# Where the inverse roots of a normalisation are worked out: on 112 x 4 numbers and spread by products, or on all 128 x 448 at once

## The chip, the cores and the metric

The kernel runs on one core of one Trainium2 chip. The metric is the device time of one execution in microseconds (us), median over several runs. TensorE multiplies matrices and writes its sums to PSUM; VectorE, ScalarE and GpSimd work element by element (GpSimd not in PSUM); SyncE issues the transfers. Every engine takes its instructions strictly in the order in which the program lists them, and waits at an instruction whose input or output buffer is not ready.

## The reference, cut to what matters

Three stages follow one another: a sigmoid attention with 4 batches of 448 tokens and 12 heads, a gated feed-forward block with a root-mean-square normalisation in front (768 to 1536 to 768), and a routed block with 8 experts. The change lies in the normalisation.

```python
def _moe_ref(x, w_gate, w_val, w_out, rms_g):            # x: 1792 tokens x 768
    rms = np.sqrt(np.mean(x * x, axis=-1, keepdims=True) + 1e-06)
    xn = x / rms * rms_g
    g = xn @ w_gate
    silu = g * (1.0 / (1.0 + np.exp(-g)))
    val = xn @ w_val
    return (silu * val @ w_out)
```

## The kernel before, in words

One batch of 448 tokens is one step of the whole. Activations stand with their features on the partitions and the tokens along a row: `xt` is six tiles of 128 x 448. Each token therefore needs one factor, 1 / root of its mean square, and that factor has to stand on all 128 partitions before a tile can be multiplied by it.

The feed-forward block of batch b (`moe1(b)`) is written as 72 pieces of nine products each: 48 pieces for gate and value, then 24 pieces for the six output chunks, four pieces to a chunk. One chunk is 36 products into one PSUM bank (lines 297, 298, 299: each value and each weight is split into a high and a low part, and three of the four partial products are taken). After every piece one step of the attention of batch b + 1 is put into the program (`attention_due`), and `later(n, ...)` puts work n pieces further on. The order on every engine is thus fixed by the code, and nothing is reordered at run time.

In the output chunks these instructions belong together. Each chunk leaves PSUM through line 338 (ScalarE, high part `x2s`), line 341 (VectorE, low part) and line 344 (VectorE, a transposed copy, the last reader of the bank). The logits (line 383, two short products) read both parts one chunk later. The next weights are split by line 250 (ScalarE, `wh`) and line 253 (VectorE, `wl`), two pairs per chunk, and line 299 reads `wl`. While batch 0 is in `moe1`, VectorE also turns 64-bit weight words into 32-bit ones (lines 219, 223, 227).

The attention of a batch ends with the normalisation, which for batches 1 to 3 lies beside the output chunks of the batch before it: about 200 to 230 us (first place), 378 to 405 us (second place) and 552 to 579 us (third place). Batch 0 has its own, at 50 us. The sums of squares per partition are in `ss` (128 x 448). Four products with `ss` as the stationary operand and a column of ones add over the partitions and leave 112 x 4 sums (`pm`, line 773). VectorE makes a first guess of 1 / root from the bits (lines 778 to 786); three Newton steps follow, by GpSimd for batches 1 to 3 (lines 793 to 796). VectorE copies the 112 x 4 factors 128 times side by side (`yb`, line 801), and four products with an identity matrix bring them to all partitions in PSUM (`prs`, line 805). Line 814 multiplies the six tiles, line 817 (ScalarE) takes the high part and line 808 (VectorE) the low part.

Of the kernel before, what the change touches and what calls it, by code (L numbers as in the profile page):

```python
# [9 lines left out]
F32 = mybir.dt.float32  # L10
F32R = mybir.dt.float32r
F16 = mybir.dt.float16
I32 = mybir.dt.int32
AF = mybir.ActivationFunctionType
ALU = mybir.AluOpType
# [4 lines left out]
B, H, S, D = 4, 12, 448, 64  # L20
NT = B * S
DM = H * D
# [6 lines left out]
CT = 112  # L29
NC = S // CT  # L30
# [66 lines left out]
def f32(ap):  # L97
    return ap.bitcast(F32)
# [3 lines left out]
def block_kernel(ctx, tc, qkp, qk, v, wg, wv, wo, g, gate, w1, w2, consts, out):  # L102
    nc = tc.nc
    ctx.enter_context(tc.manual_schedule())

    def opened(name, side="left", **kw):
        s = ExitStack()
        return s, s.enter_context(tc.tile_pool(name=name, bufs=1, side=side, **kw))
# [8 lines left out]
    s_a, aq = opened("aq", side="right", reuse_waits="tile")  # L117
# [6 lines left out]
    def const(name, parts=128):  # L124
        a, n = CONST[name]
        return cst[:parts, a : a + n]

    ident = const("ident")
    ones = cpool.tile([128, 128], F32, name="ones")
# [3 lines left out]
    start = cpool.tile([128, 1], F32, name="start")  # L133
# [15 lines left out]
    def bank(tag, bufs, shape, name):  # L149

        if tag not in fixed:
            return ps.tile(shape, F32, tag=tag, name=name, bufs=bufs)
        t = fixed[tag].pop(0)
        fixed[tag].append(t)
        n = math.prod(shape[1:])
        t = t[: shape[0], :n]
        return t if len(shape) == 2 else t.rearrange("p (a b) -> p a b", b=shape[2])
# [30 lines left out]
    sc_bank = lambda shape, name: bank("sc", 2, shape, name)  # L188
# [351 lines left out]
    def attention(b):  # L540
# [25 lines left out]
        def low(t):  # L566
            h, c = divmod(t, NC)
            a, ah = a_t[t]
            if c == 3:
                nc.vector.tensor_tensor(out=ah[64:128], in0=a[64:128], in1=f32(ah[64:128]), op=ALU.subtract)  # L570
                al = None
            else:
                al = aq.tile([128, S], F32R, tag="al", name="al", bufs=3)
                nc.vector.tensor_tensor(out=al, in0=a, in1=f32(ah), op=ALU.subtract)
            a_t[t] = ah, al
# [162 lines left out]
        for t in range(n_steps + 4 if b > 1 else 0):  # L738
            if t < n_steps:
                h, c = divmod(t, NC)  # L740
# [27 lines left out]
            step()  # L768
            yield

        pm = sc_bank([CT, NC], "pm")
        for c in range(NC):
            nc.tensor.matmul(pm[:, c : c + 1], ss[:, c * CT : (c + 1) * CT], ones[:, 0:1], start=True, stop=True)
        yield
        va = aq.tile([CT, NC], F32, tag="va", name="va")
        ya = aq.tile([CT, NC], F32, tag="ya", name="ya")
        ta = aq.tile([CT, NC], F32, tag="ta", name="ta")
        nc.vector.tensor_scalar(out=va, in0=pm, scalar1=1.0 / DM, scalar2=1e-6, op0=ALU.mult, op1=ALU.add)

        nc.vector.tensor_scalar(  # L780
            out=ta.bitcast(I32), in0=va.bitcast(I32), scalar1=1, scalar2=None, op0=ALU.logical_shift_right
        )
        nc.vector.tensor_scalar(
            out=ya.bitcast(I32), in0=ta.bitcast(I32), scalar1=-1.0, scalar2=float(0x5F3759DF), op0=ALU.mult, op1=ALU.add
        )
        nc.vector.tensor_scalar(out=va, in0=va, scalar1=-0.5, scalar2=None, op0=ALU.mult)
        for _ in range(3):
            if b == 0:
                nc.vector.tensor_tensor(out=ta, in0=ya, in1=ya, op=ALU.mult)
                nc.vector.tensor_tensor(out=ta, in0=ta, in1=va, op=ALU.mult)  # L790
                nc.vector.scalar_tensor_tensor(out=ya, in0=ta, scalar=1.5, in1=ya, op0=ALU.add, op1=ALU.mult)
            else:
                nc.gpsimd.tensor_tensor(out=ta, in0=ya, in1=ya, op=ALU.mult)
                nc.gpsimd.tensor_tensor(out=ta, in0=ta, in1=va, op=ALU.mult)
                nc.gpsimd.tensor_scalar(out=ta, in0=ta, scalar1=1.5, scalar2=None, op0=ALU.add)
                nc.gpsimd.tensor_tensor(out=ya, in0=ya, in1=ta, op=ALU.mult)
        if b > 0:
            yield
            yield
        yb = aq.tile([CT, NC, 128], F32, tag="yb", name="yb")  # L800
        nc.vector.tensor_copy(out=yb, in_=ya.unsqueeze(2).to_broadcast([CT, NC, 128]))
        yield
        pr = sc_bank([128, S], "prs")
        for c in range(NC):
            nc.tensor.matmul(pr[:, c * CT : (c + 1) * CT], yb[:, c, :], ident[:CT, :CT], start=True, stop=True)
        yield
        def low(c, xh, xl):
            nc.vector.tensor_tensor(out=xl, in0=xt[c], in1=f32(xh), op=ALU.subtract)  # L808

# [1 line left out]
        for c in range(KD):  # L811
# [3 lines left out]
                out=xt[c], in0=xt[c], scalar=g_sb[:, c : c + 1], in1=pr, op0=ALU.mult, op1=ALU.mult  # L815
# [366 lines left out]


    att = {b: attention(b) for b in range(B)}
    for n in range(H // 2 * NC + 2):
        next(att[0])
# [6 lines left out]
        if n == 15:  # L1193
            nc.scalar.copy(out=gate_2[:, :, :E], in_=gate_sb)
            nc.vector.tensor_tensor(
                out=gate_2[:, :, E:], in0=gate_sb, in1=f32(gate_2[:, :, :E]), op=ALU.subtract
# [12 lines left out]
    for b in range(B):  # L1209
# [3 lines left out]
        for n, _ in enumerate(moe1(b)):  # L1213
# [5 lines left out]
            if b == 0:  # L1219
                if to_store:  # L1220
                    c, w = to_store.pop(0)
# [186 lines left out]
```

## Time and profile before

| | |
|---|---|
| median of 3 runs | 988.81 us (988.07 to 988.83) |
| the profiled execution | 988.29 us, of it 986.2 us from the first to the last instruction |
| TensorE busy | 963.8 us, 98% |
| VectorE busy | 637.2 us, 65% |
| ScalarE busy | 463.6 us, 47% |
| GpSimd busy | 14.9 us, 2% |
| mean granted TensorE clock | 0.998 of full speed |

Busy shares are averages over stages that are bound in different ways; what a change in one stage does has to be read in that stage. A row of the timeline gives start, duration, engine, line, operation, output and inputs, and in brackets the idle time of the engine ahead of it with what ended it. A product's duration is longer than its distance to the next one, because products overlap.

### The profile page before, as it was taken

How to read it: one execution, taken by the hardware profiler on the slowest of the kernel's cores; microseconds unless marked ns; L12 is line 12 of the kernel's file. 1: busy time of each engine (PE TensorE's matmuls, PEld its weight loads, DVE VectorE, ACT ScalarE, POOL GpSimd, SP SyncE). 2: the span in 40 equal slices, each digit the busy share in tenths (PEclk: the TensorE clock that was granted, in tenths of full speed). 3: DMA queues.
4: the chain of work that ended last, by engine and by line, in shares of the span. 5: the costliest groups of instructions: out<-in, count | busy, mean ns of one | idle time of the engine just before them, and what ended most of it. 6: DMA issues, size and time to landing. Idle time of an engine off the chain costs nothing.

```text
span 986.2 us, 14474 instructions
## 1 busy us (share of the span) xinstructions
PE 963.8 (98%) x5334; PEld 829.0 (84%) x5334; DVE 637.2 (65%) x1103; ACT 463.6 (47%) x776; POOL 14.9 (2%) x43
## 2 busy tenths in 40 slices
PE   8989999989999999999999999999999999999996
PEld 3467766777999999899999988999889988889996
DVE  5778866787798774779877465654446744444454
ACT  6743443424788872578877233332322232232230
POOL 0000000020000001000000100000000000000000
PEclk9999999999999999999999999999999999999999
DMA  8949653677544435644342569433577659838632
GB/s 323 341 166 350 243 192 119 211 244 228 184 123 138 154 101 165 195 167 126 124 144 80 143 219 319 129 99 129 142 220 235 199 172 370 296 113 289 170 65 52
DMA packets 121457, 184.33 MB, mean 187 GB/s; under 512 B 62538, under 2 KB 79690, under 8 KB 121377
## 3 DMA queue, kind: packets, MB, share of 16 engines
q1 hardware_dynamic: 119344, 182.55, 57.3%
q8 instruction: 44, 0.72, 0.3%
q0 software_dynamic: 144, 0.53, 0.2%
q10 hardware_dynamic: 1888, 0.23, 0.2%
q14 instruction: 37, 0.30, 0.1%
HBM read 145.26 MB, written 37.88 MB: 186 GB/s over the span
## 4 chain that ended last, share of the span: by engine, by line
PE 85%; DVE 6%; DMA 4%; ACT 1%; issue 1%; SPq 1%; POOL 1%; DVEq 0%; ACTq 0%
PE mm L297 19%; PE mm L298 19%; PE mm L299 19%; PE sc L297 4%; PE sc L298 4%; PE sc L299 4%; PE pav L584 2%; PE psc L551 2%; PE psc L657 2%; PE psc L552 2%; PE pav L686 2%; PE pav L586 1%; DMA xd<-x2s 1%; DVE wl L253 1%; DVE xl L808 1%
## 5 line engine op out<-in xcount | busy, mean ns | idle before, releaser
L297 PE MATMUL mm<-xh,wh 128*128 128x448 f32 x576 | 213.5, 371 | 1.3 <-ACT xh L817 1.0
L298 PE MATMUL mm<-xl,wh 128*128 128x448 f32 x576 | 210.8, 366 | 0.2 <-DVE xl L808 0.2
L299 PE MATMUL mm<-xh,wl 128*128 128x448 f32 x576 | 210.1, 365 | 0.0
L253 DVE TENSOR_TENSOR wl<-w,wh 128x768 fp32r<-128x768 f32 x126 | 119.5, 948 | 30.8 <-ACT wh L250 26.4
L250 ACT CAST wh<-w 128x768 fp32r<-128x768 f32 x126 | 105.5, 838 | 52.7 <-PE mm L298 23.2
L297 PEld LDWEIGHTS mm<-xh,wh 128*128 128x128 f32 x576 | 108.2, 188 | 24.5 <-issue 9.6
L298 PEld LDWEIGHTS mm<-xl,wh 128*128 128x128 f32 x576 | 108.2, 188 | 8.8 <-DVE xl L808 0.5
L299 PEld LDWEIGHTS mm<-xh,wl 128*128 128x128 f32 x576 | 108.2, 188 | 8.7
L297 PE MATMUL mm<-hs,wh 128*128 128x448 f32 x288 | 106.3, 369 | 0.3 <-DVE xr L344 0.3
L299 PE MATMUL mm<-hs,wl 128*128 128x448 f32 x288 | 105.4, 366 | 0.1
L298 PE MATMUL mm<-hs,wh 128*128 128x448 f32 x288 | 105.5, 366 | 0.0
L297 PE MATMUL sc<-hh,w2h 128*128 128x448 f32 (+1 forms) x200 | 72.0, 360 | 0.5 <-DVE yt L910 0.5
L298 PE MATMUL sc<-hl,w2h 128*128 128x448 f32 (+1 forms) x200 | 71.2, 356 | 0.0
L299 PE MATMUL sc<-hh,w2l 128*128 128x448 f32 (+1 forms) x200 | 71.2, 356 | 0.0
L297 PE MATMUL mm<-xd,w1h 128*128 128x448 f32 x192 | 70.8, 369 | 0.0
L298 PE MATMUL mm<-xd,w1h 128*128 128x448 f32 x192 | 70.1, 365 | 0.0
L299 PE MATMUL mm<-xd,w1l 128*128 128x448 f32 x192 | 70.1, 365 | 0.0
L561 ACT ACTIVATE a<-psc,logs 128x448 f32<-128x448 f32 x96 | 61.4, 640 | 15.7 <-PE psc L552 12.0
L891 ACT ACTIVATE hh<-mm 128x448 fp32r<-128x448 f32 x32 | 17.4, 544 | 105.2 <-PE mm L299 105.2
L563 ACT ACTIVATE ah<-psc,logs 128x448 fp32r<-128x448 f32 x96 | 60.9, 635 | 0.0
L297 PEld LDWEIGHTS mm<-hs,wh 128*128 128x128 f32 x288 | 54.1, 188 | 7.9 <-issue 1.9
L299 PEld LDWEIGHTS mm<-hs,wl 128*128 128x128 f32 x288 | 54.1, 188 | 5.2 <-DVE wl L253 0.5
(214 smaller groups left out, 1569.3 us busy)
## 6 DMA issues: line engine op xcount, KB each, us to landing
w<-w32d SPq DMA_DIRECT2D x108, 384.0 KB, 4.1
w1r<-in_w SPq DMA_DIRECT2D x24, 512.0 KB, 7.2
w2r<-in_w SPq DMA_DIRECT2D x32, 384.0 KB, 6.5
rqk<-in_qk SPq DMA_DIRECT2D x24, 480.0 KB, 3.7
x2s<-x2s SPq DMA_DIRECT2D x48, 224.0 KB, 2.0
xd<-x2s SPq DMA_DIRECT2D x8, 1344.0 KB, 11.7
w<-in_wg SPq DMA_DIRECT2D x12, 768.0 KB, 6.6
w<-in_wv SPq DMA_DIRECT2D x12, 768.0 KB, 6.6
```

What stands on the lines that cost most here:

```text
L250: nc.scalar.copy(out=h, in_=w3)
L253: nc.vector.tensor_tensor(out=l, in0=w3, in1=f32(h), op=ALU.subtract)
L297: nc.tensor.matmul(p, wh, xh, start=(n == 0), stop=False)
L298: nc.tensor.matmul(p, wh, xl, start=False, stop=False)
L299: nc.tensor.matmul(p, wl, xh, start=False, stop=last)
L551: nc.tensor.matmul(psc, kh[:, keys], q2, start=True, stop=False)
L552: nc.tensor.matmul(psc, kl[:, keys], q2, start=False, stop=True)
L561: nc.scalar.activation(out=a, in_=psc, bias=logs, **act)
L563: nc.scalar.activation(out=ah, in_=psc, bias=logs, **act)
L584: nc.tensor.matmul(pav[h], v2[:, c, :], ah, start=(c == 0), stop=(c == 3))
L657: nc.tensor.matmul(to, r[h, k : k + D], r[h, :S], start=True, stop=True)
L686: nc.tensor.matmul(sums[p][i][h], v4[o, c, x, :], a[x if c < NC - 1 else 0][o], start=(c == 0), stop=(c == (NC - 1 if i == x else NC - 2)),)
```

## The change

For batches 1 to 3 the sums are made by one product with a 128 x 128 square of ones as the stationary operand and `ss` as the moving one: its 128 x 448 result holds every token's sum on every partition. The first guess and the three Newton steps then run on all 128 x 448 elements, all by VectorE, into tiles in SBUF (`va` in the place of `tmp`, `ss` itself as scratch, the factors in the place of `yb`). GpSimd, the copy `yb` and the products `prs` are gone. The number of steps between the last attention step and the scaling stays five. Batch 0 is unchanged.

```diff
+        def start_root(va, ta, ya, p):
+            nc.vector.tensor_scalar(out=va, in0=p, scalar1=1.0 / DM, scalar2=1e-6, op0=ALU.mult, op1=ALU.add)
+            nc.vector.tensor_scalar(
+                out=ta.bitcast(I32), in0=va.bitcast(I32), scalar1=1, scalar2=None, op0=ALU.logical_shift_right
+            )
+            nc.vector.tensor_scalar(
+                out=ya.bitcast(I32), in0=ta.bitcast(I32), scalar1=-1.0, scalar2=float(0x5F3759DF),
+                op0=ALU.mult, op1=ALU.add,
+            )
+            nc.vector.tensor_scalar(out=va, in0=va, scalar1=-0.5, scalar2=None, op0=ALU.mult)
+
+        def newton(va, ta, ya):
+            nc.vector.tensor_tensor(out=ta, in0=ya, in1=ya, op=ALU.mult)
+            nc.vector.tensor_tensor(out=ta, in0=ta, in1=va, op=ALU.mult)
+            nc.vector.scalar_tensor_tensor(out=ya, in0=ta, scalar=1.5, in1=ya, op0=ALU.add, op1=ALU.mult)
+
-            else:
-                nc.gpsimd.tensor_tensor(out=ta, in0=ya, in1=ya, op=ALU.mult)
-                nc.gpsimd.tensor_tensor(out=ta, in0=ta, in1=va, op=ALU.mult)
-                nc.gpsimd.tensor_scalar(out=ta, in0=ta, scalar1=1.5, scalar2=None, op0=ALU.add)
-                nc.gpsimd.tensor_tensor(out=ya, in0=ya, in1=ta, op=ALU.mult)
...
+        else:
+
+            yield
+            pm = sc_bank([128, S], "pm")
+            nc.tensor.matmul(pm, ones, ss, start=True, stop=True)
+            yield
+            va = aq.tile([128, S], F32, tag="tmp", name="va")
+            pr = aq.tile([128, S], F32, tag="yb", name="ya")
+            start_root(va, ss, pr, pm)
+            for _ in range(3):
+                yield
+                newton(va, ss, pr)
```

In the changed file the first guess is on lines 772 to 780, the Newton step on lines 783 to 785, the product with ones on line 808, the scaling on line 824 and its low part on line 818.

On VectorE at the first place, these rows stood in the program before:

```order
L223 SCALAR_TENSOR_TENSOR w_1865<-w_1823,w_1865 128x768
L778 TENSOR_SCALAR va<-pm 112x4
L780 TENSOR_SCALAR ta<-va 112x4
L783 TENSOR_SCALAR ya<-ta 112x4
L786 TENSOR_SCALAR va<-va 112x4
L227 SCALAR_TENSOR_TENSOR w_1865<-w_1823,w_1865 128x768
L253 TENSOR_TENSOR wl<-w_1828,wh 128x768
L219 TENSOR_SCALAR w_1941<-w_1859 128x768
L223 SCALAR_TENSOR_TENSOR w_1941<-w_1859,w_1941 128x768
L801 COPY yb<-ya 112x512
L227 SCALAR_TENSOR_TENSOR w_1941<-w_1859,w_1941 128x768
L341 TENSOR_TENSOR x2s<-mm_124,x2s 128x448
```

After the change the same stretch of VectorE's program is this, up to the second Newton step (the third follows four rows later):

```order
L227 SCALAR_TENSOR_TENSOR w_1865<-w_1823,w_1865 128x768
L772 TENSOR_SCALAR va<-pm 128x448
L773 TENSOR_SCALAR ss<-va 128x448
L776 TENSOR_SCALAR ya<-ss 128x448
L780 TENSOR_SCALAR va<-va 128x448
L253 TENSOR_TENSOR wl<-w_1828,wh 128x768
L219 TENSOR_SCALAR w_1925<-w_1859 128x768
L223 SCALAR_TENSOR_TENSOR w_1925<-w_1859,w_1925 128x768
L783 TENSOR_TENSOR ss<-ya 128x448
L784 TENSOR_TENSOR ss<-ss,va 128x448
L785 SCALAR_TENSOR_TENSOR ya<-ss,ya 128x448
L227 SCALAR_TENSOR_TENSOR w_1925<-w_1859,w_1925 128x768
```

The four small rows became four of 448 elements, one row further back, and the copy became three such rows for each Newton step; everything else kept its order.

On VectorE at the second place, this is the end of the normalisation before, up to the first scalings:

```order
L786 TENSOR_SCALAR va<-va 112x4
L253 TENSOR_TENSOR wl<-w_3722,wh 128x768
L801 COPY yb<-ya 112x512
L341 TENSOR_TENSOR x2s<-mm_124,x2s 128x448
L344 STREAM_TRANSPOSE xr<-mm_124 128x14x32
L253 TENSOR_TENSOR wl<-w_3754,wh 128x768
L814 SCALAR_TENSOR_TENSOR xt<-xt,g_sb,prs 128x448 x2
```

And this is what stands there after the change:

```order
L780 TENSOR_SCALAR va<-va 128x448
L783 TENSOR_TENSOR ss<-ya 128x448
L784 TENSOR_TENSOR ss<-ss,va 128x448
L785 SCALAR_TENSOR_TENSOR ya<-ss,ya 128x448
L341 TENSOR_TENSOR x2s<-mm_124,x2s 128x448
L344 STREAM_TRANSPOSE xr<-mm_124 128x14x32
L253 TENSOR_TENSOR wl<-w_3740,wh 128x768
L783 TENSOR_TENSOR ss<-ya 128x448
L784 TENSOR_TENSOR ss<-ss,va 128x448
L785 SCALAR_TENSOR_TENSOR ya<-ss,ya 128x448
L783 TENSOR_TENSOR ss<-ya 128x448
L784 TENSOR_TENSOR ss<-ss,va 128x448
```

The first Newton step stands ahead of the exit of the chunk (lines 341 and 344), the other two behind it and ahead of the scalings; the `wl` that stood ahead of the copy now stands ahead of the first guess.

On TensorE at the second place, the four `pm` products stood ahead of the last piece of a chunk:

```order
L299 MATMUL mm_124<-hs,wl 128x448
L773 MATMUL pm<-ones,ss 112x1 x4
L297 MATMUL mm_124<-hs,wh 128x448
L298 MATMUL mm_124<-hs,wh 128x448
L299 MATMUL mm_124<-hs,wl 128x448
```

The one product with the square of ones stands behind that piece and the logits, ahead of the next chunk:

```order
L299 MATMUL mm_124<-hs,wl 128x448
L383 MATMUL mm_123<-x2s,gate_83 16x448 x2
L808 MATMUL pm<-ss,ones 128x448
L297 MATMUL mm_125<-hs,wh 128x448
L298 MATMUL mm_125<-hs,wh 128x448
```

The sums are asked for one piece, and at the second place also the two logit products, later than before; the four `prs` products in the middle of the next chunk are gone.

## Rows read from the trace of the kernel before

**Rows 1.** Windows: us, busy us of PE, PEld, DVE, ACT, POOL; PEclk; DMA share; GB/s.

```profile
216.00:226.00 10.00, 10.00 (x51) 8.85 (x49) 9.96 (x17) 3.83 (x7) 0.00 (x0) 1.00 0.33 120
395.00:405.00 10.00, 10.00 (x50) 8.77 (x49) 9.95 (x17) 5.95 (x11) 0.00 (x0) 1.00 0.28 78
...
980.00:986.00 6.00, 0.00 (x0) 0.00 (x0) 0.00 (x0) 0.00 (x0) 0.00 (x0) 0.69 0.17 30
```

**Rows 2.** Timeline of TensorE at the first place: start us, us, instruction, idle before it.

```profile
203.28 0.92 PE L773 MATMUL pm<-ones,ss 128*112 128x1 f32 x8 [0.85 <-DVE ss L604]
...
213.69 1.12 PE L805 MATMUL prs<-cst,yb 112*128 112x112 f32 x8 [1.63 <-DVE yb L801]
...
222.84 0.37 PE L299 MATMUL mm<-hs,wl 128*128 128x448 f32 x1
...
228.89 0.44 PE L297 MATMUL mm<-hs,wh 128*128 128x448 f32 x1 [0.27 <-DVE xr L344]
```

**Rows 3.** Timeline of VectorE at the first place.

```profile
213.12 0.43 DVE L801 COPY yb<-ya 112x512 f32<-112x512 f32 x1 [2.97 <-POOL ya L796]
...
221.71 0.95 DVE L253 TENSOR_TENSOR wl<-w,wh 128x768 fp32r<-128x768 f32 x1
...
228.10 0.64 DVE L344 STREAM_TRANSPOSE xr<-mm 128x448 f32<-128x448 f32 x1
```

**Rows 4.** Timeline of VectorE at the second place, and one row of the third.

```profile
385.06 0.16 DVE L778 TENSOR_SCALAR va<-pm 112x4 f32<-112x4 f32 x1 [4.09 <-PE pm L773]
385.25 0.17 DVE L780 TENSOR_SCALAR ta<-va 112x4 int32<-112x4 int32 x1
...
385.61 0.95 DVE L253 TENSOR_TENSOR wl<-w,wh 128x768 fp32r<-128x768 f32 x1
389.80 0.43 DVE L801 COPY yb<-ya 112x512 f32<-112x512 f32 x1 [3.25 <-POOL ya L796]
...
393.76 1.27 DVE L814 SCALAR_TENSOR_TENSOR xt<-xt,g_sb,prs 128x448 f32<-128x448 f32 x2 [1.60 <-PE prs L805]
...
402.20 0.92 DVE L253 TENSOR_TENSOR wl<-w,wh 128x768 fp32r<-128x768 f32 x1
...
576.43 0.92 DVE L253 TENSOR_TENSOR wl<-w,wh 128x768 fp32r<-128x768 f32 x1
```

**Rows 5.** Timeline of TensorE at the second place, and one row of the third.

```profile
384.16 0.86 PE L773 MATMUL pm<-ones,ss 128*112 128x1 f32 x8
384.88 0.46 PE L297 MATMUL mm<-hs,wh 128*128 128x448 f32 x1
...
387.22 0.36 PE L297 MATMUL mm<-hs,wh 128*128 128x448 f32 x1
...
392.68 1.04 PE L805 MATMUL prs<-cst,yb 112*128 112x112 f32 x8
393.49 0.45 PE L297 MATMUL mm<-hs,wh 128*128 128x448 f32 x1
...
404.05 0.36 PE L299 MATMUL mm<-hs,wl 128*128 128x448 f32 x1
...
578.28 0.36 PE L299 MATMUL mm<-hs,wl 128*128 128x448 f32 x1
```

**Rows 6.** Groups by shape: line, engine, operation, count, busy us, mean ns.

```profile
L574 DVE TENSOR_TENSOR al<-a,ah 128x448 fp32r<-128x448 f32 x72 | 44.7, 620 | 7.6 <-ACT ah L563 7.4
L892 DVE SCALAR_TENSOR_TENSOR hl<-mm,hh 128x448 fp32r<-128x448 f32 x32 | 20.0, 624 | 59.0 <-ACT hh L891 58.8
L219 DVE TENSOR_SCALAR w<-w 128x768 int32<-128x768 int32 x18 | 10.0, 554 | 0.3 <-DMA w<-in_wv 0.3
L1140 DVE TENSOR_SCALAR s_idf<-mi 128x56 f32<-128x56 f32 x1 | 0.2, 213 | 0.0
L686 PE MATMUL pav<-aj,rv 64*64 64x448 f32 x42 | 11.2, 540 | 0.0
L1044 PE MATMUL av<-cst,hr 128*128 128x128 f32 x6 | 1.1, 271 | 0.0
```

More of the change, by code (lines that the diff above doesn't have):

```diff
@@ L769, in attention @@
             yield
[L771 to L791, printed above, removed]
-            else:
-                nc.gpsimd.tensor_tensor(out=ta, in0=ya, in1=ya, op=ALU.mult)
-                nc.gpsimd.tensor_tensor(out=ta, in0=ta, in1=va, op=ALU.mult)
-                nc.gpsimd.tensor_scalar(out=ta, in0=ta, scalar1=1.5, scalar2=None, op0=ALU.add)
-                nc.gpsimd.tensor_tensor(out=ya, in0=ya, in1=ta, op=ALU.mult)
@@ L797, in attention @@
-        if b > 0:
-            yield
-            yield
[L800 to L806, printed above, removed]
+        def start_root(va, ta, ya, p):
[8 more added lines that the diff above has]
+            nc.vector.tensor_scalar(out=va, in0=va, scalar1=-0.5, scalar2=None, op0=ALU.mult)
@@ new lines, in newton @@
+        def newton(va, ta, ya):
+            nc.vector.tensor_tensor(out=ta, in0=ya, in1=ya, op=ALU.mult)
+            nc.vector.tensor_tensor(out=ta, in0=ta, in1=va, op=ALU.mult)
+            nc.vector.scalar_tensor_tensor(out=ya, in0=ta, scalar=1.5, in1=ya, op0=ALU.add, op1=ALU.mult)
+        if b == 0:
+            pm = sc_bank([CT, NC], "pm")
+            for c in range(NC):
+                nc.tensor.matmul(pm[:, c : c + 1], ss[:, c * CT : (c + 1) * CT], ones[:, 0:1], start=True, stop=True)
+            yield
+            va, ta, ya = (aq.tile([CT, NC], F32, tag=n, name=n) for n in ("va", "ta", "ya"))
+            start_root(va, ta, ya, pm)
+            for _ in range(3):
+                newton(va, ta, ya)
+            yb = aq.tile([CT, NC, 128], F32, tag="yb", name="yb")
+            nc.vector.tensor_copy(out=yb, in_=ya.unsqueeze(2).to_broadcast([CT, NC, 128]))
+            yield
+            pr = sc_bank([128, S], "prs")
+            for c in range(NC):
+                nc.tensor.matmul(pr[:, c * CT : (c + 1) * CT], yb[:, c, :], ident[:CT, :CT], start=True, stop=True)
+            yield
[7 more added lines that the diff above has]
+            start_root(va, ss, pr, pm)
+            for _ in range(3):
+                yield
+                newton(va, ss, pr)
```

## The prediction

> **What bounds the kernel now.** The page gives TensorE 98% of the span, so the windows over the three places come first [rows 1]. From 216 to 226 us TensorE is busy 10.00 of 10 us, and so, almost, is VectorE: 9.96; from 395 to 405 it is 10.00 and 9.95. The reader is to see that the 65% of the whole span hides stretches of ten microseconds in which VectorE has no room.
>
> The timeline of TensorE at the first place shows what ended its waits [rows 2]: 0.85 us for `ss` ahead of `pm`, 1.63 us for `yb` ahead of `prs`, and 0.27 us at 228.89 for line 344, the last reader of the bank. The timeline of VectorE there [rows 3] has one gap, 2.97 us ahead of the copy `yb`, in which it waits for GpSimd. At the other two places TensorE does not wait.
>
> So the number that decides is how far VectorE may slip before TensorE sees it. Line 299 needs the `wl` of line 253. At the first place that row starts at 221.71 and lasts 0.95 [rows 3], and line 299 starts at 222.84 [rows 2]: 0.18 us of slack; at 228.89 there is none. At the second, 402.20 + 0.92 = 403.12 [rows 4] against 404.05 [rows 5]: 0.93 us. At the third, 576.43 + 0.92 = 577.35 [rows 4] against 578.28 [rows 5]: 0.93 us again. Both rows of line 253 stand behind the normalisation in VectorE's program.
>
> **Prices on VectorE.** A product or a fused product of two 448-element tiles takes 0.62 us (lines 574 and 892 [rows 6]). An operation of one tile with constants takes 0.554 us for 768 elements in SBUF (line 219 [rows 6]) and 0.16 for four [rows 4]; on the line between them 448 elements take 0.39. Out of PSUM 56 elements take 0.213 (line 1140 [rows 6]), some 1 ns for each beyond the four: 0.61 for 448. An operation that waits for the one before starts 0.03 to 0.04 us after its end (385.06 + 0.16 to 385.25 [rows 4]); one that doesn't starts 0.08 before it (two scalings of 0.676 take 1.27 [rows 4]).
>
> First guess, start to start: 0.65 + 0.43 + 0.31 + 0.31 = 1.70 us. A Newton step: 0.66 + 0.66 + 0.54 = 1.86, or 1.98 where the next row waits for its result. Bounds: the one unsure price is whether the three SBUF operations of the first guess go at line 219's rate; at that of line 574 they cost 0.23 more each, 0.7 per batch. If the one that reads PSUM went at line 219's rate, it would be 0.2 less. I take the values above, since these are nearest in kind.
>
> Taken away: the four small rows, 385.06 to 385.61 = 0.55 us [rows 4], of which some 0.1 comes back at the first place because line 227 then waits for line 223 directly; and the copy, 0.43 - 0.08 = 0.35.
>
> **Prices on TensorE.** `pm` costs 384.88 - 384.16 = 0.72 [rows 5], and the product behind it is 0.46 long instead of 0.36, so 0.81 in all; `prs` likewise 0.81 + 0.09 = 0.90. The new product is recorded twice, like every product of full-precision operands (eight records for four products [rows 5]). A record of 448 columns lasts 0.540, one of 128 lasts 0.271 [rows 6]: 0.84 ns a column, or 0.38 us for 448, so 0.75 for both and 0.09 behind: 0.84. Bounds: 0.4 (two products at 0.2, since 51 of them fill 10.00 us [rows 1]) and 1.1 (two whole records). TensorE thus does 0.81 + 0.90 - 0.84 = 0.87 us less per batch. GpSimd's rows cost nothing to drop except the waits for them, already counted.
>
> **First place.** VectorE gets 1.70 + 1.86 + 1.86 + 1.98 = 7.40 us more and 0.45 + 0.35 less, net 6.6. The sums come in time, since line 227 is still running. The 2.97 us gap is filled, as nothing waits for GpSimd any more. Left: 6.6 - 2.97 = 3.6 us. Line 253 moves from 221.71 to 225.3 and line 344 from 228.10 to 231.7. TensorE saves 0.85, 1.63 and 0.87 on the way and arrives early at line 299, but it waits there until 225.3 + 0.95 = 226.3; the 16 products behind take 3.3 us at 0.2 each, to 229.6, and then it waits again, for the logits' low part (line 341) and for line 344, until 232.4. The next chunk starts at 232.5 instead of 228.89: **+3.6 us**. From there ScalarE, VectorE and the transfers that VectorE's rows release are late by the same amount, so no later slack gives it back.
>
> **Second place.** The product with ones now stands behind the last piece and the logits: it starts where 387.22 [rows 5] stands less the 0.81 of `pm`, at 386.41, and its sums can be read 0.75 + 0.16 (a record's 0.54 less its 0.38) later and a start of 0.04 behind, at 387.35, instead of 385.06. From there: first guess 1.70; one Newton step 1.86; lines 341, 344 and 253, which take their 1.94 us as before (from the end of `yb` at 390.23 to 393.76 - 1.60 [rows 4]); two Newton steps 1.98 each. The first scaling starts at 396.8 instead of 393.76: 3.1 us late, although VectorE has more than 7 us of idle in this place (4.09 + 3.25 + 1.60 [rows 4]), because what was parallel waiting is now a chain behind a later product. The rows behind the scalings keep their order, so line 253 ends at 403.12 + 3.1 = 406.2, and line 299 starts 2.2 us after its 404.05. TensorE, 0.87 us less work behind it, stands still for about 3. **+2.2 us.** A new product cheaper or dearer by 0.3 moves this by as much.
>
> **Third place.** Its rows lie as at the second, with the same slack: **+2.2 us**.
>
> Sum: 3.6 + 2.2 + 2.2 = 8.0 us. Against the profiled execution's own 988.29 (span 986.2 and 2.1 around it) that is 996.3; the median of the runs is 0.5 above that execution. I forecast 996.5.
>
> **A falling clock.** In the stretch 980 to 986, where TensorE runs nothing, its granted clock is 0.69 of full speed [rows 1]: part of it was spent at the lower level, 1.2 GHz. In 216 to 226, soon after the 1.63 us wait, it is 1.00. At the first place TensorE would stand still for 4 us (about 222 to 226.3). If the clock fell there, the 16 products would take 6.6 us instead of 3.3, to 232.9, and the next chunk would start some 1 us later than at 232.5, up to 3 if its own products begin slowly too: 9 to 11 us in all.
> The Trainium skill ("TensorE: Matmul & The Clock Gate", section "HAM oscillation — how this bites in real kernels") warns of this: gaps between groups of products put the clock back to its half rate, and each group then starts cold. By that rule the sum is 9 to 11 us, by the rows of this trace 8.0, since no wait inside the kernel shows a drop.
>
> **The rivals.**
> - *VectorE stays ahead (faster).* If line 253 is in time at all three places, only what TensorE no longer does is left: 3 x 0.87 + 0.85 + 1.63 = 5.1 us less, 983.4. This is decided by the duration of the thirteen operations. At the second and third place they would have to take 2.2 us less than 7.4, at the first 3.6 less, so 0.3 us each instead of 0.57. For it speaks nothing but that no row shows this chain; against it every 448-element row in the trace. 10%.
> - *Only the first place binds.* If the product with ones comes sooner or the first guess is cheaper than I take it, and the slack at places two and three is enough, they give -0.87 each: 3.6 - 1.7 = +1.9, 990.4. Needed is a slip of 0.9 instead of 3.1 there. 12%.
> - *The gain and the loss cancel.* With all thirteen operations at line 219's rate (0.39) the first place slips by 1.3 and the others by 0.8, under their slack: 1.3 - 2 x 0.1 = +1.1, no change that can be told. 8%.
> - *The clock falls* as above: 998 to 999.5. 13%.
> - The forecast, each place bound by VectorE: its own range follows from the bounds of the prices, 0.7 more per batch in the first guess (+2.1) down to 0.2 less there and 0.3 less in the product (-1.3): 995 to 998.6. 57%.
>
> **How the numbers follow.** The range reaches from the case in which only the first place binds to the falling clock: 990.2 to 999.5. Below it lie the faster case and the cancelling one. A change of 0.2%, 2 us, is about what measurements of this kernel can tell from none. Faster: the first rival, 0.10. Same: the cancelling case and half of the one that binds at the first place alone, since +1.9 lies at that bound, 0.14. Slower: the rest, 0.76.
>
> **What the changed profile would show.** Lines 772 to 785 as rows of 0.62, 0.39, 0.39, 0.39 and then 0.62 nine times per batch; line 808 as two records of 0.54; no GpSimd rows before 700 us. Among the waits of TensorE, those for `yb` and `ss` gone, and new ones for line 253 (some 4 us at the first place), line 341 and line 344. VectorE without a gap from 200 to 230 us. At the second place the distance from the first guess to the first scaling should be 9.5 us and TensorE should stand still for about 3 us before line 299 at what was 404.05. The forecast is wrong if TensorE shows no wait for `wl`, if the thirteen operations take clearly less than 7.4 us, or if the waits are there but shorter because something ahead of them was late too.

## The result and the profile after

The changed kernel takes 996.48 us (median of six runs, 996.08 to 998.61) against 988.68 (987.82 to 989.46): a ratio of 1.0085, 95% interval 1.0072 to 1.0098, or 7.8 us more. The forecast was 996.5. The execution shown here took 998.05 us; its span is 996.0 at a mean granted clock of 0.993. Three of the six runs have spans of 994.0 to 994.2, the other three of 995.0 to 996.6.

The page's first part, after (busy us, share, instructions):

```profile
PE 966.4 (97%) x5292; PEld 827.0 (83%) x5292; DVE 656.0 (66%) x1127; ACT 463.9 (47%) x776; POOL 3.5 (0%) x7
```

TensorE is busy 2.6 us more and the span is 9.8 longer, so most of the loss is waiting. TensorE's waits in the changed kernel (us in total, times, longest):

```profile
PE mm L383 <- DVE x2s L341: 5.7, 4, 1.8
...
PE mm L299 <- DVE wl L253: 3.7, 3, 2.7
```

The wait for `yb` ahead of `prs` and the one for `ss` ahead of `pm` at the first place [rows 2] are gone; VectorE's late rows stand in their place. Not all of the 5.7 us for line 341 is new. The kernel before has this at the end of the first place, ahead of the 228.89 of [rows 2]:

```profile
226.79 0.37 PE L383 MATMUL mm<-x2s,gate 128*16 128x448 f32 x1 [0.55 <-ACT x2s L338]
228.24 0.38 PE L383 MATMUL mm<-x2s,gate 128*16 128x448 f32 x1 [1.07 <-DVE x2s L341]
```

The thirteen operations, as groups by shape (count, busy us, mean ns):

```profile
L784 DVE TENSOR_TENSOR ss<-ss,va 128x448 f32<-128x448 f32 x9 | 5.6, 625 | 0.3
L785 DVE SCALAR_TENSOR_TENSOR ya<-ss,ya 128x448 f32<-128x448 f32 x9 | 5.6, 625 | 0.3
L783 DVE TENSOR_TENSOR ss<-ya 128x448 f32<-128x448 f32 x9 | 5.6, 618 | 0.1
L808 PE MATMUL pm<-ss,ones 128*128 128x448 f32 x6 | 2.7, 538 | 0.0
L772 DVE TENSOR_SCALAR va<-pm 128x448 f32<-128x448 f32 x3 | 1.9, 622 | 6.5 <-PE pm L808 6.5
L776 DVE TENSOR_SCALAR ya<-ss 128x448 int32<-128x448 int32 x3 | 1.2, 395 | 0.1
```

These are the prices of the prediction, the unsure one too: the SBUF operations of the first guess take 0.39 us, the rate of line 219 and not that of line 574 [rows 6].

**First place.** VectorE, to be held against [rows 3]:

```profile
207.31 0.62 DVE L772 TENSOR_SCALAR va<-pm 128x448 f32<-128x448 f32 x1
...
220.28 1.28 DVE L824 SCALAR_TENSOR_TENSOR xt<-xt,g_sb,ya 128x448 f32<-128x448 f32 x2
...
225.27 0.95 DVE L253 TENSOR_TENSOR wl<-w,wh 128x768 fp32r<-128x768 f32 x1
...
231.68 0.64 DVE L344 STREAM_TRANSPOSE xr<-mm 128x448 f32<-128x448 f32 x1
```

The gap of 2.97 us is filled, line 253 starts at 225.27 (forecast 225.3) and line 344 at 231.68 (231.7). TensorE, against [rows 2]:

```profile
216.58 0.38 PE L383 MATMUL mm<-x2s,gate 128*16 128x448 f32 x1 [1.76 <-DVE x2s L341]
...
218.51 0.57 PE L297 MATMUL mm<-hs,wh 128*128 128x448 f32 x1
218.89 0.57 PE L298 MATMUL mm<-hs,wh 128*128 128x448 f32 x1
...
226.28 0.47 PE L299 MATMUL mm<-hs,wl 128*128 128x448 f32 x1 [2.66 <-DVE wl L253]
...
232.47 0.44 PE L297 MATMUL mm<-hs,wh 128*128 128x448 f32 x1 [0.27 <-DVE xr L344]
```

The next chunk starts at 232.47 instead of 228.89: 3.58 us late, and so is line 344. VectorE has no gap between the rows shown, nor has it in the kernel before from its copy `yb` to line 344, so its lateness reaches the next chunk in full. Behind the wait of 1.76 us eight products follow one another at 0.37 us, not 0.2, but TensorE then waits for line 253 anyhow, so that costs nothing.

**Second and third place.** VectorE at the second (against [rows 4]):

```profile
390.89 0.62 DVE L772 TENSOR_SCALAR va<-pm 128x448 f32<-128x448 f32 x1 [3.25 <-PE pm L808]
...
400.33 1.28 DVE L824 SCALAR_TENSOR_TENSOR xt<-xt,g_sb,ya 128x448 f32<-128x448 f32 x2
...
408.77 0.92 DVE L253 TENSOR_TENSOR wl<-w,wh 128x768 fp32r<-128x768 f32 x1
```

From the first guess to the first scaling it takes 9.44 us (forecast 9.5). TensorE at the second, then at the third place, against [rows 5]:

```profile
403.19 0.47 PE L299 MATMUL mm<-hs,wl 128*128 128x448 f32 x1 [0.52 <-DVE wl L253]
...
408.34 0.38 PE L383 MATMUL mm<-x2s,gate 128*16 128x448 f32 x1 [1.45 <-DVE x2s L341]
408.99 0.44 PE L297 MATMUL mm<-hs,wh 128*128 128x448 f32 x1 [0.27 <-ACT x2s L338]
...
409.74 0.47 PE L299 MATMUL mm<-hs,wl 128*128 128x448 f32 x1
...
584.85 0.38 PE L383 MATMUL mm<-x2s,gate 128*16 128x448 f32 x1 [1.38 <-DVE x2s L341]
...
586.24 0.69 PE L299 MATMUL mm<-hs,wl 128*128 128x448 f32 x1
586.73 0.57 PE L297 MATMUL mm<-hs,wh 128*128 128x448 f32 x1
```

Line 299 stands at 409.74 instead of 404.05, 5.69 us later, and TensorE had come in 3.51 late: 2.18 at this place. At the third it is 586.24 instead of 578.28, 7.96 less the 5.79 it came in with: 2.17. Behind it the products run at 0.37 again, and this time nothing waits behind them. The windows (columns as in [rows 1]; the clock is the third from the end):

```profile
215.00:220.00 5.00, 3.09 (x8) 2.21 (x9) 4.90 (x9) 0.00 (x0) 0.00 (x0) 0.77 0.49 191
...
395.00:405.00 10.00, 9.48 (x47) 8.21 (x46) 9.75 (x17) 1.97 (x5) 0.00 (x0) 1.00 0.30 102
585.00:590.00 5.00, 4.62 (x14) 3.66 (x14) 3.12 (x5) 1.13 (x2) 0.00 (x0) 0.66 0.80 174
```

At a granted clock of 0.66 part of 585 to 590 was spent at 1.2 GHz. TensorE is 9.71 us late behind it, so 1.75 came from the clock. What VectorE's lateness adds at a place is called its slip here: 3.58 + 2.18 + 2.17 = 7.9, and with the clock's 1.75 it makes 9.7 of the 9.8 us by which this span is longer. Smaller differences behind it cancel: 0.4 comes back up to 620 us, and 0.5 is added behind the last product.

### The profile page after: what moved, and what is told of

Read it like the earlier page. It is cut to its first block, busy times and chain, and to the rows that moved or that the text cites. A ratio compares the mean times of both kernels' runs of the same rounds, so it can differ in the third digit from the quotient of the medians.

```text
span 996.0 us, 14376 instructions
## 1 busy us (share of the span) xinstructions
PE 966.4 (97%) x5292; PEld 827.0 (83%) x5292; DVE 656.0 (66%) x1127; ACT 463.9 (47%) x776; POOL 3.5 (0%) x7
## 4 chain that ended last, share of the span: by engine, by line
PE 86%; DVE 9%; ACT 2%; issue 1%; DMA 1%; DVEq 0%; ACTq 0%
PE mm L297 19%; PE mm L299 19%; PE mm L298 19%; PE sc L297 4%; PE sc L299 4%; PE sc L298 4%; PE pav L686 3%; PE psc L657 3%; PE pav L584 2%; PE psc L551 2%; PE psc L552 2%; PE pav L586 1%; DVE wl L253 1%; DVE xt L824 1%; DVE xl L818 1%
## 5 line engine op out<-in xcount | busy, mean ns | idle before, releaser
L299 PE MATMUL mm<-hs,wl 128*128 128x448 f32 x288 | 107.4, 373 | 4.1 <-DVE wl L253 3.7
L297 PE MATMUL mm<-hs,wh 128*128 128x448 f32 x288 | 108.3, 376 | 1.1 <-ACT x2s L338 0.5
L298 PE MATMUL mm<-hs,wh 128*128 128x448 f32 x288 | 106.5, 370 | 0.0
```

Source lines behind the costliest of these rows:

```text
L297: nc.tensor.matmul(p, wh, xh, start=(n == 0), stop=False)
L298: nc.tensor.matmul(p, wh, xl, start=False, stop=False)
L299: nc.tensor.matmul(p, wl, xh, start=False, stop=last)
```

## The experiments

The theory: VectorE works in order, the thirteen long operations make lines 253, 341 and 344 late, and each place pays what its slack and its gap do not cover. The rivals: the loss comes from the clock; from one place that delays the others; or from the new place of the product with ones.

For each trace the table gives how much later (us) than in the trace of before the same product starts: what is added inside each place (at 228.89, 404.05 and 578.28 of before, less what that trace had at 202.06, 377.98 and 552.01), and what is added behind it up to the next (377.98, 552.01, 597.02), then near 600 (597.02 to 619.91). What differs ahead of the first place (up to 1.1 us) and behind 620 us (under 1 us) is left out, so a row need not add up to the time of its execution. The last column is the median less that of the kernel before, run beside it.

| kernel | first | behind | second | behind | third | behind | near 600 | medians |
|---|---|---|---|---|---|---|---|---|
| the change | 3.58 | -0.07 | 2.18 | 0.10 | 2.17 | 1.68 | -0.33 | +7.8 |
| e1 batch 1 only | 3.57 | 0.11 | -0.14 | 0.13 | -0.13 | 0.04 | -0.20 | +1.6 |
| e5 batch 1 only | 3.59 | -0.01 | -0.01 | 0.02 | -0.01 | 0.01 | 0.24 | +2.9 |
| e2 batches 2, 3 | 0.39 | 1.17 | 2.18 | 1.74 | 2.18 | 1.67 | -0.31 | +6.6 |
| e6 batches 2, 3 | 0.02 | 0.08 | 2.18 | 0.11 | 2.17 | 1.52 | -0.28 | +7.1 |
| e3 two steps | 1.59 | 1.39 | 0.20 | 0.10 | 0.20 | 0.86 | 1.26 | +3.4 |
| e10 four steps | 5.61 | 0.00 | 4.16 | 0.11 | 4.16 | 0.14 | 1.65 | +13.9 |
| e4 product and guess early | 3.33 | 1.43 | 0.79 | 0.68 | 0.78 | 0.16 | 1.08 | +5.6 |
| e7 product early | 3.58 | 0.37 | -0.08 | 0.09 | -0.07 | 0.12 | 1.09 | +4.3 |
| e8 mix | -0.03 | 0.25 | -0.08 | 0.08 | -0.08 | 0.12 | 1.12 | +0.6 |
| e9 product two pieces early | 0.48 | 1.46 | -0.91 | -0.02 | -0.91 | 0.01 | 0.84 | -1.4 |
| e11 before again | 0.04 | -0.05 | 0.00 | -0.04 | 0.00 | 0.01 | 0.95 | one run |

**The places apart.** The diffs of this section are cut to what matters and stand against the changed kernel unless said otherwise. In e1 and e2 the old branch also gets its GpSimd rows back:

```diff
-        if b == 0:            # old way
+        if b != 1:            # e1; e2: if b < 2
...
```

> The new way for batch 1 alone, the old way for batches 2 and 3. If VectorE's late rows are the cause and each place costs what its own slack does not cover, the first place alone gives +3.6 us: about 992.3 against 988.7, TensorE waiting for line 253 about 2.7 us and for line 341 about 1.1 there, and no wait for VectorE in 395 to 412. If the loss comes mostly from a granted clock that falls behind such waits, only the part that is seen at the first place stays (the clock fell there in 215 to 225 in the changed kernel, but TensorE then waited anyhow), and later_two carries the rest. If the places hang together, so that the later two are late only because the first one is, this kernel alone gives nearly the whole +8.

> The new way for batches 2 and 3 alone, the old way for batch 1. Late rows: +2.2 at each of two places, 4.4 in all: about 993.1, with a wait of some 1.4 us for line 341 at each, and up to 1.7 more in an execution in which the granted clock falls behind the third place's wait. If the places hang together: near 988.7. With the kernel that changes the first place alone the two losses should add up to the 8 of the whole change.

Measured: e1 990.85 against 989.22 (ratio 1.0016, 1.0007 to 1.0026), e2 995.78 (1.0070, 1.0056 to 1.0083). By the traces each place costs the same alone as in the whole change, so they do not hang together (the -0.14 and -0.13 of e1 come with an empty step that it has less for batches 2 and 3; e5 has -0.01). The medians do not split so: 1.6 instead of 3.6, 6.6 instead of 4.4, though their sum is 8.2. In e2 the clock fell behind both waits (0.83 over 405 to 415 and 583 to 593), 1.74 and 1.67 us; it also had one empty step less than the kernel before for batch 1, whose copy therefore came early and whose first place was not the old one. (The 1.17 us behind that place is no fallen clock, as the expectation of e6 below has it: the granted clock is 1.00 from 230 to 250 us; 0.49 of it is a wait for line 344.) Both were repeated with all steps:

```diff
             if b > 0:
                 yield
+                yield
             yb = ...
```

> The new way for batch 1 alone once more; batches 2 and 3 take the old way with all of its empty steps (in the run e1_first_place they had one step less). Slip theory: the trace shows the chunk behind the first place 3.6 us late and nothing at the other two places, as the trace of e1 did (3.58). The median of e1 was only 1.6 us over the kernel before, while its traced execution was 2.4 us over its own median relative to that of before; if that was the spread of single executions, the median lies 1.6 to 3.6 over the kernel before, 990.7 to 992.6. If the clock rival is at work in the kernel before as well, in most of its executions, the next two runs, whose first places are free of the new way, show a fallen clock behind the wait for the copy.

> The new way for batches 2 and 3, batch 1 exactly as in the kernel before (in e2_later_two its copy stood one step early, which made a wait of 2.5 us for line 253 at the first place and a fallen clock behind it). Slip theory: 2.2 us late at each of the two places, 4.4, and the first place as before: 993.1 to 993.6. Clock theory on top: up to 1.7 more behind each of the two waits, as e2's trace showed (windows behind both at 0.80 to 0.86), so up to 996.5. If the median comes out at 995.5 or more, the waits cost more by the clock than the prediction put down; at 993.5 or less, they do not.

Measured: e5 991.54 against 988.65 (1.0031, 1.0019 to 1.0043), e6 995.79 (1.0071, 1.0057 to 1.0085). In the traces the slips are 3.59 and 2.18 + 2.17 again. The trace of e6, its shortest execution (993.35), lost 1.52 by the clock behind the third place alone; its other four lie 1.4 to 2.5 us higher. So slip is 4.4 of e6's 7.1, and by the traces the clock is what can make up the rest; which places lost it in the four executions without a trace here is not shown. The two medians add up to 10.0 this time, against 7.8 for the whole change: the medians alone don't show the sum to better than 2 us.

**The duration of the rows.** One Newton step less (e3), one more (e10):

```diff
-            for _ in range(3):
+            for _ in range(2):      # e3, then one empty step
                 yield
                 newton(va, ss, pr)
+            newton(va, ss, pr)      # e10, with range(3)
```

> The whole change, but with two Newton steps instead of three, the third is left out (its place in the program stays empty), so the factors are less exact. VectorE does 1.9 to 2.0 us less per batch. If the duration of the operations is the cause: first place 3.6 - 1.9 = 1.7, the other two 1.1 us late at the scalings against 0.93 of slack, so 0.2 each: +2.1, about 990.8. If it is the place of the product with ones (one piece later than before) that costs, or the mere exchange of the engine, little changes: 995 to 996.5.

> The whole change with a fourth Newton step of three more rows right behind the third, the suspected cost made larger. With every slack used up, each further step of 1.97 us per batch should be paid in full at all three places: 8.0 + 5.9 = 13.9 over the kernel before, 1002.6; two, three and four steps then lie on 2.1, 8.0 and 13.9 by slip alone. With the clock falling behind the longer waits, up to 1.7 at each of the later two places: up to 1006. If the cost were the changed order or the missing small rows and not the rows' time: 996 to 998.

Measured: e3 992.66 against 989.22 (1.0034, 1.0021 to 1.0048), e10 1003.19 against 989.33 (1.0145, 1.0130 to 1.0161). The slips at the three places are 1.59, 0.20, 0.20 with two steps (forecast 1.7, 0.2, 0.2), 3.58, 2.18, 2.17 with three, and 5.61, 4.16, 4.16 with four (5.6, 4.2, 4.2). That is 1.97 to 2.03 a step wherever the slack is used up. The rows' time is the cause; neither the exchange of engines nor the order alone would scale like this. The median of e3 is 1.3 us above what was expected (3.4 over the kernel before, not 2.1); its trace has 1.39 from the clock behind the first place (0.66 in 230 to 235 us) and 1.26 near 600 us (below).

**The place of the product.**

```diff
         else:
-            yield
             pm = sc_bank([128, S], "pm")
             nc.tensor.matmul(pm, ones, ss, start=True, stop=True)
             yield
+            yield                   # e7; in e4 behind the Newton steps instead
             va = aq.tile(...)
```

> The whole change, but the product with ones and the first guess stand one piece of nine products earlier, where the old sums stood; as many steps as before follow. At the second and third place the sums can be read some 2.2 us sooner, the scalings are 0.8 instead of 3.1 us late, under the slack of 0.93: no wait there, and TensorE does 0.87 less in each, so 3.6 - 1.7 = +1.9: about 990.6. At the first place VectorE has no gap, so nothing changes there: +3.6. If the thirteen operations alone make the loss, wherever they stand, 995 to 996.5.

> The whole change, but with only the product with ones one piece earlier; the first guess keeps its place in the program, behind line 253. e4, which also moved the first guess, put that row of line 253 (0.87 us) into the chain from the sums to the scalings, so that they came 1.7 us late instead of 0.8. Slip theory: here 0.8 late at the second and third place, within the slack of 0.93, no wait for line 253 there and 0.87 less work each: 3.6 - 1.7 = +1.9 without the clock, up to +3.2 with a fallen clock behind the first place (e4's trace lost 1.2 there): 990.6 to 992. If thirteen operations of 448 elements cost what they cost wherever the product stands: 995 to 996.5.

Measured: e4 994.82 against 989.22 (1.0053, 1.0040 to 1.0067), e7 992.93 against 988.65 (1.0043, 1.0029 to 1.0056): both above what was expected. The trace of e4 also lost 1.43 us (not 1.2) by a fallen clock behind the first place. VectorE of e4 at the second place shows the part that the edit caused:

```profile
390.55 0.39 DVE L780 TENSOR_SCALAR va<-va 128x448 f32<-128x448 f32 x1
390.85 0.95 DVE L253 TENSOR_TENSOR wl<-w,wh 128x768 fp32r<-128x768 f32 x1
391.72 0.62 DVE L783 TENSOR_TENSOR ss<-ya 128x448 f32<-128x448 f32 x1
...
399.46 1.28 DVE L824 SCALAR_TENSOR_TENSOR xt<-xt,g_sb,ya 128x448 f32<-128x448 f32 x2
```

A row of line 253 that had run while VectorE waited for the sums now stands between guess and Newton: 0.87 us more in the chain, and a slip of 0.79 at each of the two places. e7 keeps the guess behind that row. There it waits for the product (first row), and at the end line 253 meets line 299 almost exactly:

```profile
389.19 0.63 DVE L772 TENSOR_SCALAR va<-pm 128x448 f32<-128x448 f32 x1 [0.99 <-PE pm L807]
...
407.06 0.92 DVE L253 TENSOR_TENSOR wl<-w,wh 128x768 fp32r<-128x768 f32 x1
```

```profile
408.04 0.47 PE L299 MATMUL mm<-hs,wl 128*128 128x448 f32 x1
```

407.06 + 0.92 = 407.98, and line 299 starts at 408.04. The scalings are 0.8 late as expected, and TensorE loses nothing; but it does not gain 0.87 either. The slack of 0.93 was counted from the old time of line 299. A TensorE that does less comes earlier and uses that slack up itself: what a place costs is the lateness less 0.93, and no less than -0.87. Here 0.81 - 0.93 = -0.12, measured -0.08.

In the trace of before the squares were ready 7 us before the sums' first product, so e9 puts the product with ones two pieces early, for batches 2 and 3 alone; batch 1 is as in the kernel before:

```diff
         while steps_due:
             step()
-            yield
+            if b < 2 or steps_due:
+                yield
...
             nc.tensor.matmul(pm, ones, ss, start=True, stop=True)
+            yield
+            yield
             yield
```

> Batch 1 as in the kernel before; batches 2 and 3 by the new way with the product with ones two pieces earlier than in the change (the squares were added up 7 us before the product in the trace of before). In e7 the first guess had waited 0.99 us for the product, behind line 253; without that wait the scalings come 0.2 us early instead of 0.8 late, line 253 is in time, and TensorE keeps the 0.87 us that it does less: -1.7 for the two places. In e3, e4, e7 and e8 TensorE then waited 1.1 to 1.3 us near 600 us for line 405, behind weights that came late by a transfer; if this takes back what is gained, -0.6. So 987.0 to 988.1 against 988.7. If VectorE's rows still hold TensorE up at line 253, 988.5 to 989.5.

Measured: 987.92 against 989.33, ratio 0.9986 (0.9977 to 0.9995), 1.4 us less than the kernel before, by less than 0.2%, and the only version here that is faster than it. Each place gives -0.91 (forecast -0.87). Between 378 and 415 us TensorE waits for nothing. VectorE's guess starts with no wait, right behind line 253:

```profile
383.96 0.96 DVE L253 TENSOR_TENSOR wl<-w,wh 128x768 fp32r<-128x768 f32 x1 [2.19 <-ACT wh L250]
384.84 0.62 DVE L773 TENSOR_SCALAR va<-pm 128x448 f32<-128x448 f32 x1
```

**The gap at the first place.**

```diff
-                nc.gpsimd...            # four rows, three times (against the kernel before)
+                newton(va, ta, ya)      # 112 x 4, VectorE, batch 1
...
```

> Batch 1 as in the kernel before, but its Newton steps on the 112 x 4 numbers go by VectorE instead of GpSimd (nine small rows of 0.2 us in place of a gap of 2.97); batches 2 and 3 by the new way with the product with ones one piece earlier, as in e7. Slip theory: the gap of 2.97 us at the first place becomes 1.8 of work, so the copy and the wait of TensorE behind it come 1.1 us sooner and nothing takes it back: -1.1; the other two places -0.8 each. Together -2.7: about 986. If the first place is bound by something other than VectorE's rows, or the other two wait after all: 988.5 to 991.

Measured: 989.22 against 988.65 (1.0009, 1.0000 to 1.0018): nothing gained. The later two places give -0.08 each, as in e7, and not -0.8. At the first place the copy comes 1.3 us sooner (211.81 instead of 213.12 [rows 3]), as expected, but VectorE loses it three rows on:

```profile
213.01 0.62 DVE L341 TENSOR_TENSOR x2s<-mm,x2s 128x448 fp32r<-128x448 f32 x1
214.85 0.65 DVE L344 STREAM_TRANSPOSE xr<-mm 128x448 f32<-128x448 f32 x1 [1.23 <-DMA x2d<-xr]
```

Line 344 waits for the transfer that still reads its single buffer. TensorE, which waits only 0.28 us for `yb` now, waits for line 253 instead, and the next chunk starts at 228.89 as before:

```profile
222.71 0.47 PE L299 MATMUL mm<-hs,wl 128*128 128x448 f32 x1 [1.10 <-DVE wl L253]
```

The gap of 2.97 us was hiding this transfer too; the change's longer rows hid it as well. A second buffer was not tried.

**The kernel before once more.**

> The kernel before, unchanged, for a second trace: is its first execution shown here (span 986.2, no fallen clock) typical? If single executions of it lose about a microsecond somewhere, as the medians of 988.7 to 989.2 suggest, its rows lie up to 1 us later from some place on: at the first place if the clock falls behind the wait of 1.63 us for the copy, near 600 us if it is the wait for late weights, or spread evenly.

Measured: 988.33 us, span 986.2, the clock 1.00 at every place. Near 600 us it differs from the first trace:

```profile
606.29 0.44 PE L297 MATMUL mm<-xh,wh 128*128 128x448 f32 x1 [1.00 <-DVE r_lg L405]
```

Line 405 stands behind a row of VectorE whose weights come by a transfer. This microsecond comes and goes with that transfer in the unchanged kernel as well, so the 0.8 to 1.7 of the column "near 600" is not put down to any edit. And e9, whose first place is written as before, shows a fallen clock there:

```profile
225.00:230.00 5.00, 2.98 (x10) 1.60 (x9) 4.79 (x8) 1.83 (x4) 0.00 (x0) 0.90 0.62 197
230.00:235.00 5.00, 5.00 (x21) 4.53 (x20) 1.49 (x2) 1.90 (x3) 0.00 (x0) 0.76 0.94 191
```

It cost 1.46 us, behind the three waits that end the first place (0.58, 1.06 and 0.28 us). The first trace of before has the same three (0.55, 1.07 and 0.27) at 1.00. The changed kernel has them too (0.58, 1.06 and 0.27). In the traces of e3 and e4 the clock fell behind them as well (1.39 and 1.43), while in those of the change, e1, e5, e7 and e10 it fell only earlier in the place, where that was hidden. So either way can lose some 1.4 us here. Of the 46 executions of the kernel before that ran beside the experiments, the 18 with a mean granted clock of 0.996 or less took 989.5 us on average, the 28 with more 988.7. That fits e1 and e5, 3.6 in both traces and 1.6 and 2.9 in the medians; that it is the whole of that difference is not shown.

## Why the prediction was right

- **What bounds the kernel now.** Right: VectorE's slack decided all three places, the 0.93 of line 253 at the second and third [rows 4 and 5] and, at the first, the slack of nothing at 228.89. The prediction's list of TensorE's waits there leaves out the 0.55 for line 338 and the 1.07 for line 341, so a wait for line 341 there is no new sign by itself. The slack was counted against TensorE's old times, which is right where VectorE is late, and in the rival in which gain and loss cancel (0.8 late, -0.1 each). It is wrong for the rival in which only the first place binds: scalings 0.8 us late make -0.08 at a place, not -0.87 (e7). The full 0.87 needs a lateness of 0.06 or less (e9). The fastest rival counts 0.85 and 1.63 us of TensorE's waits at the first place as gained, which e8 contradicts.
- **Prices on VectorE.** Right: 0.62, 0.39, and 0.62 for the Newton rows; 1.97 to 2.03 per further step against 1.98.
- **Prices on TensorE.** The saving of 0.87 per batch was 0.91 (e9).
- **First place.** Right: 3.58 against 3.6, with line 253, line 344 and the next chunk at the forecast times. That the 2.97 us are filled holds. The wait for line 253 is 2.66 us and not some 4, because the wait of 1.76 for line 341 and the slow products behind it came first. By its last sign, waits that are shorter because something ahead was late too, the prediction would have been wrong here; but the slip is set by line 344 and was not changed by it. That shorter work in the gap would be a gain, as e8 expected, does not hold.
- **Second place, third place.** Right in sum, 2.18 and 2.17 against 2.2. Line 253 ends at 408.77 + 0.92 = 409.69, and line 299 starts at 409.74. TensorE stands still for 2.18 + 0.87 = 3.05 us, the forecast 3, but not in one wait ahead of line 299: 0.52 for `wl`, 1.45 for line 341 and 0.27 for line 338, because the whole stretch of VectorE's rows is late, and the rest in wider distances between the products around these waits.
- **A falling clock.** Here a term was too small. It was set at nothing because no wait inside the traced kernel showed a drop, and was looked for behind the longest wait at the first place. In the trace after it fell behind the shorter one there (1.76 us, hidden) and behind the third place, where it cost 1.75. In e7 it did fall behind the longest wait:

```profile
226.41 0.74 PE L299 MATMUL mm<-hs,wl 128*128 128x448 f32 x1 [2.65 <-DVE wl L253]
```

```profile
225.00:230.00 5.00, 3.59 (x10) 3.21 (x11) 5.00 (x9) 1.67 (x4) 0.00 (x0) 0.50 0.39 130
```

The prediction priced that at 1 to 3 us; the slip there is 3.58 as without it, because the slow products end before VectorE's rows do. The clock falls in some executions and places and not in others. That the medians still differ by 7.8, next to a slip of 7.9, fits a kernel before that loses time by it as well, but is not shown.
- **The number.** 996.48 against 996.5 is partly luck: single executions took 996.08 to 998.61, the traced one lost 1.75 to a clock that was set at nothing, and e5 and e6 add up to 10.0. What the traces bear out is the slip of 7.9 against 8.0.

The Trainium skill ("TensorE: Matmul & The Clock Gate", section "HAM oscillation — how this bites in real kernels") shows a kernel whose products start at the half rate behind each long wait for a transfer. Behind the third place the trace shows such a start, a window of 0.66 behind a wait of 1.38 us; at the second place of the same trace, behind 1.45 us, the clock is 1.00 from 395 to 415. So here the fall was not certain, and it came behind waits for VectorE.

## What to carry to other kernels

Before work is moved to the engine that a full stretch waits for, read its slack at the place, row by row, and add up the rows that stand ahead of the next deadline in its program: that sum gave each place's slip within 0.1 us. Slack and saved work are not added: an engine that becomes faster comes earlier and uses the slack up itself. A chain of long rows is hidden only if its input is made early enough, and a move of two pieces was worth 3.1 us at each of two places here (2.18 to -0.91).

## What the runs showed of the hardware

In the changed kernel the clock fell behind waits of 1.4 to 1.8 us (0.77 in 215 to 220, 0.66 in 585 to 590) and stayed at 1.00 behind the longer one of 2.66 us (225 to 230, next products at 0.2 us); in e7 it fell behind that same wait (2.65 us, 0.50), and in e9 behind three shorter ones (0.76 in 230 to 235). Each fall that was not hidden cost 1.4 to 1.7 us, some nine products at 0.37 instead of 0.2. A place written alike kept its clock in one kernel and lost it in another (second place, 405 to 415: e6 1.00, e2 0.83). So no wait in these traces tells by its length alone whether the clock falls behind it.
